# A long convolution with a spectral mix on one core: another layout for the last sequence's u, an earlier identity load and fewer zero columns

## The chip, the cores and the metric

The kernel runs on one core of one Trainium2 chip. The metric is the device time of one execution in microseconds (us), and a time shown alone is the median of its runs. The engines are called as in the profile: PE (TensorE, matrix multiplication), PEld (its weight loads), DVE (VectorE), ACT (ScalarE), POOL (GpSimd) and SP (SyncE, which here issues DMA transfers only). PSUM is the memory that TensorE writes to; an "evacuation" is the copy by VectorE or ScalarE of a result from PSUM to SBUF.

## The reference

Inputs are x (8, 5696, 128), h (5696, 128), two sets of 64 complex mixing matrices (w_r and w_i, each 64, 128, 128) and w_ch (128, 128), all float32. Two functions follow each other:

```python
def _attn_ref(x, h):                       # causal long convolution
    B, S, D = x.shape
    L = 2 * S
    Xf = np.fft.rfft(x, n=L, axis=1)
    Hf = np.fft.rfft(h, n=L, axis=0)
    Yf = Xf * Hf[None, :, :]
    y = np.fft.irfft(Yf, n=L, axis=1)[:, :S, :]
    return y.astype(np.float32)

def _moe_ref(x, w_r, w_i, w_ch):           # x is the y from above
    B, S, D = x.shape
    n_modes = w_r.shape[0]                 # 64
    X = np.fft.rfft(x, axis=1)
    Y = np.zeros_like(X)
    Xr, Xi = (np.real(X[:, :n_modes]), np.imag(X[:, :n_modes]))
    Yr = np.einsum('bmd,mde->bme', Xr, w_r) - np.einsum('bmd,mde->bme', Xi, w_i)
    Yi = np.einsum('bmd,mde->bme', Xr, w_i) + np.einsum('bmd,mde->bme', Xi, w_r)
    Y[:, :n_modes] = Yr + 1j * Yi
    y = np.fft.irfft(Y, n=S, axis=1)
    u = x + y
    return (u + np.maximum(u @ w_ch, 0.0)).astype(np.float32)
```

## The kernel before, in words

**Order and semaphores.** The kernel is a list of operations for each engine, written out by hand. A recorder (`Recorder`, L21 to L121) keeps them in the order of the program text, and works out semaphores from tokens: an operation names the tokens that it reads and writes, and with `after=` those whose earlier readers and writers must be done. There is no scheduler, so an engine runs its operations strictly in the order in which the text adds them. Helpers record nearly everything: `evac` (L304, with the ScalarE copies at L311 and L313 and the VectorE ones at L315 and L317), `dma` (L319, issue at L320) and `mm` (L322, matmul at L323). Transfers issued by SP or by POOL go out in the order of that engine.

**Sizes.** A sequence has S = 5696 = 64 x 89 positions. A position is written J·q + p with J = 64, NQ = 89 values of q and p from 0 to 63. There are NK = 90 frequency groups k, 0 to 89. The eight sequences are worked in NP = 4 pairs. The frequencies go in NT = 23 ticks (steps) of KT = 4 k each.

**First stage.** The first transform is along q. `F1` (L142) holds its 90 cosines and 90 sines as 2·NK = 180 columns, of which the imaginary ones of k = 0 and k = 89 are zero. The filter h is transformed first, in 16 tiles (`Ah`). Then `a_tile` (L461) does the same for a pair: four matmuls F, Xin of 180 columns into two PSUM banks, and one evacuation with a scale of 1/64 into `As` (128 partitions x 720 elements). A pair has 32 such tiles, and where nothing else is said VectorE and ScalarE take them by turns.

**Ticks.** `tick` (L650) does, for four k: `second` (L606), matmuls As, M of 128 columns that finish the transform; `products` (L617), the product with the transformed filter `Hs` on VectorE, into `U`; two steps later the first half of the inverse transform, U times Wc, evacuated by ScalarE into a buffer `Zs` or `Zt` and stored to DRAM (`zscr`) by a transfer on SP; and one step after that the matmuls G, Zs, which gather the 64 lowest modes of y in one PSUM bank, MB. The function `zroom` (L645) says which buffer a step uses; in the last pair, step 21 uses the buffer of step 13, so ScalarE's cast of step 21 waits until step 13's store has landed.

**Between the pairs.** While the last ticks of a pair run, tiles 0 to 5 of the next pair's first stage are put among them (`border`, L556). Tiles 6 to 31 follow between the pairs (L741): odd ones are evacuated by VectorE, even ones by ScalarE, and the last one is split between both. After them the next pair's `second` begins.

**The last pair's extra work.** Among its ticks the transfers for the output stage are issued by the dictionary `early` (L557): for example, at tick 14 `load_id` and `clear_zt(1)`, at tick 15 `load_zt(1, "gpsimd")` (1 MB, `ZT1a`), at tick 16 and 18 the tables `S4a` and `IBs`. All of these are POOL's, but for the identity matrix `Id`, which `load_id` (L568) puts on SP, with a wait (`after=ZY`) for the stores of steps 8 and 9, whose buffers lie in the same memory.

**Mix and output stage.** `mix` (L806) multiplies the modes by the weights `W`, and eight transposes with `Id` (L824) bring the result to `C`. Then `u_tile` (L787) makes u: for each sequence four chunks of 16 values of p, each chunk in two halves; a half is two PSUM banks, each with eight matmuls S4, ZT of 89 columns (the inverse transform of the convolution, read back from `zscr`) and one IBs, C of 356 columns (the mix). It is evacuated to `UT`, one 5696-column row for each of the 128 channels, with the positions in their natural order. `o_tile` (L841) makes a piece of the result: four matmuls UT, WI of 256 columns, with 128 columns of `UT` as weights each time and WI = [w_ch, identity] as the moving side, so that PSUM holds u @ w_ch beside u with positions on the partitions; ScalarE takes the maximum with 0 (L871) into `R`, VectorE adds u (L872) into `O`, and SP sends it out (L883). A sequence has eleven tiles of four groups of 128 columns, in pairs of 4 KB a row (1024 float32), and 64 positions that are left go as a short tile for two sequences together. A list `todo` (L885) deals output tiles out between the u tiles of the following pair. In the last pair all of sequence 6 comes before sequence 7, and with its last u tile twelve whole output tiles and a short one are still to be done, since every output tile of the old layout takes its columns from all four chunks:

```python
lh = bass.AP(u_sb[ub], 4 * r4 + j, [[S, P], [NW, P]])      # column 44*i + 4*r4 + j, i = 0..127
```

Of the kernel before, what the change touches and what calls it, by code (L numbers as in the profile page):

```python
# [4 lines left out]
P = 128  # L5
# [118 lines left out]
def bass_long_conv_fft__then__afno_spectral_mix_kernel(nc, x, h, moe_w_r, moe_w_i, moe_w_ch, out):  # L124
# [3 lines left out]
    J = 64  # L128
# [13 lines left out]
    f1 = np.zeros((P, 2 * NK))  # L142
    f1[0:NQ] = np.stack([fwd.real, fwd.imag], axis=2).reshape(NQ, 2 * NK)
# [105 lines left out]
    f1_sb = at("F1", 2 * NK, F16, take(2 * NK * 2))  # L249
# [13 lines left out]
    assert 2 * S + 8 * ZP <= AW * 2  # L263
# [19 lines left out]
    id_sb = at("Id", P, F16, r_off[1])  # L283
# [63 lines left out]
    R.add("scalar", lambda e: e.copy(zf, ap(f1_sb, 2 * NK, J, P - J, 1, [[0, XW // 2]])), [("f1",)], [("xz",)])  # L347
# [69 lines left out]
    dma("sync", wc_sb[:, :], bass.AP(c_w, 0, [[3 * P, P], [1, 2 * P]]), "c", (), [("wc",)])  # L417

# [13 lines left out]
    for i in range(WARM):  # L432
        mm(pv(6 + i % 2, 0, [[1, 2 * NK]]), f1_sb[:, 0:P], f1_sb[:, :], True, True, [("f1",)], [bank(6 + i % 2)])
# [6 lines left out]
    for j in range(16):  # L440
        t = turns("h", [0, 2, 4])
        for i in range(4):
            d = 4 * j + i
            mm(pv(t + i // 2, (i % 2) * 2 * NK, [[1, 2 * NK]]),
               ap(hp_sb, 2 * J * HS, 0, P, d, [[HS, 2 * J]]), f1_sb[:, :], True, True,
               [("hz",), ("hp", d // DC), ("f1",)], [bank(t + i // 2)])
        for i in range(4 if j < 15 else 26):
            mm(pv(6 + i % 2, 0, [[1, 2 * NK]]), f1_sb[:, 0:P], f1_sb[:, :], True, True, [("f1",)], [bank(6 + i % 2)])
        evac(bass.AP(ah_sb, 4 * j, [[HW, P], [DH, 2 * NK], [2, 2], [1, 2]]),
             pv(t, 0, [[1, 2 * NK], [512, 2], [2 * NK, 2]]),  # L450
             [bank(t), bank(t + 1)], [("ah", j)], 1.0 / 64,
             eng="vector" if j in (3, 7) else "scalar")
# [8 lines left out]
    def a_tile(j, slots, eng=None):  # L461
        t = turns("s", slots) if len(slots) > 1 else slots[0]
        for i in range(4):
            d = 4 * j + i
            mm(pv(t + i // 2, (i % 2) * 2 * NK, [[1, 2 * NK]]),
               ap(x_sb, XW, 0, P, d, [[XS, 2 * J]]), f1_sb[:, :], True, True,
               XIN + XZ + [("f1",)], [bank(t + i // 2)])
        if eng == "both":
            for i, e in enumerate(("vector", "scalar")):
                evac(bass.AP(a_sb, 4 * j + 2 * i, [[AW, P], [D, 2 * NK], [1, 2]]), pv(t + i, 0, [[1, 2 * NK], [2 * NK, 2]]),  # L470
                     [bank(t + i)], [("as", j + i)], 1.0 / 64, eng=e, after=once(("hp", j), HP))
            return
        evac(bass.AP(a_sb, 4 * j, [[AW, P], [D, 2 * NK], [2, 2], [1, 2]]),
             pv(t, 0, [[1, 2 * NK], [512, 2], [2 * NK, 2]]),
             [bank(t), bank(t + 1)], [("as", j)], 1.0 / 64, eng=eng, after=once(("hp", j), HP))


# [8 lines left out]
    def filter_tick(t, banks):  # L486
        n = len(ticks[t])
        hb = banks
        for i, k in enumerate(ticks[t]):
            for r in range(2):  # L490
                for dh in range(2):
                    mm(pv(hb[dh], i * DH, [[1, DH]]),
                       ap(m_sb, MW, J * dh, J, k * 3 * J + (J if r == 0 else 0) + dh * J, [[1, P]]),
                       ap(ah_sb, HW, J * dh, J, (2 * k + r) * DH, [[1, DH]]), r == 0, r == 1,
                       AHT + mtok(k) + [("ag", k)], [bank(hb[dh])])
# [54 lines left out]
    def load_s4(part):  # L550
# [9 lines left out]
             14: lambda: (load_id(), clear_zt(1)),  # L560
# [14 lines left out]
    def keep(n, b0):  # L575
        for i in range(n):
            mm(pv(b0 + i % 2, 0, [[1, 2 * NK]]), f1_sb[:, 0:P], f1_sb[:, :], True, True, [("f1",)], [bank(b0 + i % 2)])
# [28 lines left out]
    def second(g_, t):  # L606
        sl = slot_of(g_, t)
        for i, k in enumerate(ticks[t]):
            for r in range(2):
                for b in range(2):  # L610
                    col = k * 3 * J + (J if r == 0 else 0) + b * J
                    mm(pv(sl + b, i * D, [[1, D]]),
                       ap(m_sb, MW, J * b, J, col, [[1, P]]),
                       ap(a_sb, AW, J * b, J, (2 * k + r) * D, [[1, D]]), r == 0, r == 1,
                       AST + mtok(k), [bank(sl + b)])
# [139 lines left out]
    LSLOT = [0, 2, 4, 6]  # L755
    NCH = J // ZB
# [30 lines left out]
    def u_tile(i, b, half):  # L787
# [4 lines left out]
        else:  # L792
            for hb in range(2):
# [6 lines left out]
        evac(bass.AP(u_sb[ub], c_ * ZB + half * 8, [[S, P], [J, NQ], [4, 2], [1, 4]]),  # L800
             src, [bank(t), bank(t + 1)], [("u_", ub, 2 * c_ + half)], eng=e, after=once(("u", ub), old))
# [39 lines left out]
    def o_tile(g_, b, r4):  # L841
# [19 lines left out]
        n, rows = (4, P) if full else (2, TAIL)  # L861
        rd = [("u_", v_, c_) for v_ in ubs for c_ in range(2 * NCH)] + [("wch",), ("i16",)]
# [8 lines left out]
        R.add("scalar", lambda e: e.activation(rv, src_r, RELU), bk, [("r", i % NR)], after=once(("r", i % NR), G_ALL + XTT + [("y", 0), ("y", 1), ("id",)]))  # L871
# [5 lines left out]
        if full:  # L877
            dst = bass.AP(out.tensor, out.offset + bb * S * D + (4 * r4 - 4 * h_) * D, [[NW * D, P], [1, w_]])
            src = ob[:, 0:w_]
        else:  # L880
            dst = bass.AP(out.tensor, out.offset + bb * S * D + NW * P * D, [[D, TAIL], [S * D, 2], [1, D]])
            src = bass.AP(ob, 0, [[OW, TAIL], [D, 2], [1, D]])
# [56 lines left out]
```

## Time and profile before

| | |
|---|---|
| median of 3 runs | 385.36 us (384.66 to 386.22) |
| the profiled execution | 387.21 us |
| span of that execution in the trace | 385.1 us |
| mean granted TensorE clock | 0.98 |
| busy, share of the span | PE 94%, PEld 73%, DVE 77%, ACT 82%, POOL 22% |
| moved by DMA | 103.94 MB, mean 270 GB/s |
| output of u and results (290 to 372 us) | PE busy 81.93 of 82.00 us |

The profile is of one execution, somewhat slower than the median of the timed runs. The span runs from the first instruction to the last event; the 2.1 us between it and the execution's own time lie around it. Times in rows of the trace are counted from the start of the span. A row of a group gives the line, the engine, the operation with output and inputs and their shapes, the number of instructions, and in brackets the idle time of the engine just before them with what ended it. "SPq" and "POOLq" are the queues in which these engines issue transfers. The clock column is the TensorE clock that was granted, as a share of full speed.

### The profile page before, as it was taken

How to read it: one execution, taken by the hardware profiler on the slowest of the kernel's cores; microseconds unless marked ns; L12 is line 12 of the kernel's file. 1: busy time of each engine (PE TensorE's matmuls, PEld its weight loads, DVE VectorE, ACT ScalarE, POOL GpSimd, SP SyncE). 2: the span in 40 equal slices, each digit the busy share in tenths (PEclk: the TensorE clock that was granted, in tenths of full speed). 3: DMA queues.
4: the chain of work that ended last, by engine and by line, in shares of the span. 5: the costliest groups of instructions: out<-in, count | busy, mean ns of one | idle time of the engine just before them, and what ended most of it. 6: DMA issues, size and time to landing. Idle time of an engine off the chain costs nothing.

```text
span 385.1 us, 12438 instructions
## 1 busy us (share of the span) xinstructions
PE 362.4 (94%) x5346; PEld 280.7 (73%) x5346; DVE 296.6 (77%) x336; ACT 314.3 (82%) x491; POOL 85.2 (22%) x134
## 2 busy tenths in 40 slices
PE   7989899999989999999999899978999999999994
PEld 7878766667856667756667666648789989888873
DVE  3649899988988998989999988761537767766665
ACT  8469699898989997899998899965447777688884
POOL 8812012100733311823203213307200000000000
PEclk9999999999999999999999999995799999999999
DMA  7999969977999995999995799999999999999877
GB/s 148 206 298 354 243 139 249 250 220 222 97 126 215 249 268 151 132 134 232 243 274 114 95 325 357 327 367 292 392 391 362 367 416 403 419 405 383 325 293 316
DMA packets 87137, 103.94 MB, mean 270 GB/s; under 512 B 22819, under 2 KB 72611, under 8 KB 83527
## 3 DMA queue, kind: packets, MB, share of 16 engines
q1 hardware_dynamic: 62603, 67.76, 50.7%
q0 software_dynamic: 24480, 35.40, 44.2%
q8 instruction: 42, 0.69, 0.7%
q14 instruction: 12, 0.10, 0.1%
HBM read 70.61 MB, written 51.12 MB: 316 GB/s over the span
## 4 chain that ended last, share of the span: by engine, by line
PE 76%; DMA 8%; DVE 6%; ACT 4%; POOL 3%; issue 2%; DVEq 0%; ACTq 0%; POOLq 0%
PE ps L323 76%; DMA Xr<-in_x_dram 4%; DMA zscr<-Zs 3%; DVE As L317 2%; DVE U L630 2%; POOL Xr L320 2%; ACT As L313 2%; ACT R L871 1%; POOL Hin L320 1%; DVE Xin L365 1%; DVE Hs L315 1%; ACT Zt L311 1%; ACT Zs L311 0%; DMA Hs<-Hs 0%; ACT Xs L311 0%
## 5 line engine op out<-in xcount | busy, mean ns | idle before, releaser
L323 PE MATMUL ps<-U,Wc 128*128 128x512 f16 (+1 forms) x368 | 94.4, 377 | 4.2 <-ACT Zs L311 3.7
L638 DVE TENSOR_TENSOR U<-Xs,Hs 128x2048 f16<-128x2048 f16 (+1 forms) x73 | 86.9, 1192 | 13.8 <-ACT Xs L311 13.1
L311 ACT CAST Xs<-ps 128x1024 f16<-128x1024 f32 (+1 forms) x77 | 75.1, 979 | 12.6 <-PE ps L323 7.6
L311 ACT CAST Zs<-ps 128x512 f16<-128x512 f32 (+1 forms) x132 | 69.3, 592 | 5.5 <-DMA zscr<-Zs 3.8
L872 DVE TENSOR_TENSOR O<-ps,R 128x512 f32<-128x512 f32 x81 | 52.3, 685 | 20.1 <-ACT R L871 11.2
L317 DVE TENSOR_SCALAR As<-ps 128x720 f16<-128x720 f32 x70 | 57.7, 886 | 5.2 <-PE ps L323 4.6
L871 ACT ACTIVATE R<-ps 128x512 f32<-128x512 f32 (+1 forms) x92 | 50.5, 591 | 8.5 <-PE ps L323 8.4
L323 PE MATMUL ps<-F,Xin 128*128 128x180 f16 x512 | 53.7, 249 | 3.9 <-DVE Xin L365 2.6
L323 PE MATMUL ps<-As,M 64*128 64x128 f16 x1440 | 50.3, 217 | 3.5 <-DVE U L630 2.9
L323 PEld LDWEIGHTS ps<-F,Xin 128*128 128x128 f16 x512 | 44.4, 155 | 12.6 <-DVE As L317 2.8
L323 PEld LDWEIGHTS ps<-U,Wc 128*128 128x128 f16 x368 | 28.6, 97 | 33.3 <-ACT Zs L311 7.6
L313 ACT ACTIVATE As<-ps 128x720 f16<-128x720 f32 (+1 forms) x61 | 45.7, 769 | 7.9 <-PE ps L323 6.5
L323 PE MATMUL ps<-WI,UT 128*128 128x256 f16 x360 | 51.1, 278 | 0.5 <-ACT UT L311 0.4
L311 ACT CAST UT<-ps 128x712 f16<-128x712 f32 x46 | 34.5, 752 | 19.2 <-PE ps L323 18.0
L323 PEld LDWEIGHTS ps<-As,M 64*128 64x128 f16 x1440 | 40.6, 94 | 9.7 <-DVE U L630 3.6
L323 PEld LDWEIGHTS ps<-WI,UT 128*128 128x128 f16 x360 | 39.1, 152 | 3.4 <-issue 1.8
L323 PE MATMUL ps<-IBs,C 128*128 128x356 f16 x128 | 40.3, 324 | 0.1
L320 POOL DMA_DIRECT2D Xt<-in_x_dram x40 | 21.1, 533 | 80.8 <-PE ps L323 80.3
L323 PEld LDWEIGHTS ps<-G,Zs 128*128 128x128 f16 x512 | 26.3, 97 | 14.3 <-ACT Zs L311 1.6
L638 DVE TENSOR_TENSOR U<-ps,Hs 128x2048 f16<-128x2048 f32 x15 | 34.3, 2284 | 0.0
L323 PE MATMUL ps<-G,Zs 128*128 128x128 f16 (+2 forms) x512 | 32.4, 193 | 0.0
L311 ACT CAST Zt<-ps 128x512 f16<-128x512 f32 x52 | 28.5, 624 | 0.3 <-PE ps L323 0.3
(88 smaller groups left out, 504.7 us busy)
## 6 DMA issues: line engine op xcount, KB each, us to landing
out_dram<-O SPq DMA_DIRECT2D x39, 512.0 KB, 7.6
zscr<-Zs SPq DMA_DIRECT2D x62, 256.0 KB, 7.0
zscr<-Zt SPq DMA_DIRECT2D x26, 256.0 KB, 6.8
Xt<-in_x_dram POOLq DMA_DIRECT2D x20, 320.0 KB, 7.1
W<-wscr POOLq DMA_DIRECT2D x4, 1024.0 KB, 8.2
M<-cM POOLq DMA_DIRECT2D x5, 720.0 KB, 16.9
ZT0a<-zscr SPq DMA_DIRECT2D x3, 1024.0 KB, 8.8
Hs<-Hs SPq DMA_DIRECT2D x44, 64.0 KB, 6.3
```

What stands on the lines that cost most here:

```text
L311: R.add(e, lambda h_: h_.copy(dst, src), reads, writes, after=after)
L313: R.add(e, lambda h_: h_.activation(dst, src, COPY, scale=scale), reads, writes, after=after)
L315: R.add(e, lambda h_: h_.tensor_copy(dst, src), reads, writes, after=after)
L317: R.add(e, lambda h_: h_.tensor_scalar_mul(dst, src, scale), reads, writes, after=after)
L320: R.add(eng, lambda h_: h_.dma_start(dst, src), reads, writes, ring=ring, after=after)
L323: R.add("tensor", lambda h_: h_.matmul(o, l, r, start=st, stop=sp), reads, writes)
L365: R.add("vector", lambda e: e.tensor_copy(bass.AP(x_sb, i * XN * XS, [[XW, NQ], [XS, XN], [1, D]]), src), list(toks) + XZ, [("xin", i)])
L630: R.add("vector", lambda e, b=b, s_=s_: e.tensor_tensor(bass.AP(u_s[i], b * 512, [[2048, P], [1024, 2], [1, n * D]]), s_, hv, MULT), [tok, ...
L638: R.add("vector", lambda e: e.tensor_tensor(uv, src, hv, MULT), bk + [("h", t, 0), ("h", t, 1, 0), ("h", t, 1, J)], [("u", i)])
L871: R.add("scalar", lambda e: e.activation(rv, src_r, RELU), bk, [("r", i % NR)], after=once(("r", i % NR), G_ALL + XTT + [("y", 0), ("y", 1 ...
L872: R.add("vector", lambda e: e.tensor_tensor(ov, src_u, rv, ADD), bk + [("r", i % NR)], [key + (h_,)], after=once(key, old))
```

## The change

Four things are changed, and all of them keep what is computed.

1. **Zero columns.** The two zero columns of F1 are left out (NF = 178 for 180). The evacuations write from the second group of `Ah` and `As` on, and the matmuls of `second` and of the filter that multiplied by the two zero groups (k = 0 and k = 89, imaginary) are not issued.
2. **Identity.** `Id` lies in the free end of the `As` region, and is loaded by SP right behind Wc at the start, without a wait; it is no longer among the early actions at tick 14.
3. **Shares of the first stage.** Between the pairs the 25 whole tiles 6 to 30 go by a pattern of nine, five to ScalarE and four to VectorE: 14 and 11, where it was 13 and 12. The first pair's 31 whole tiles go by a string, 16 to ScalarE and 15 to VectorE, and tile 31 is split between both.
4. **The last sequence.** For sequence 7 the columns of `UT` are in another order: first by halves of p (0 to 31, 32 to 63), then by bit jh of p, then q, then four runs of four positions. One half needs chunks 0 and 1 alone, the other 2 and 3. Each half gives six output tiles, of 32, 32 and 25 values of q with two tiles each; a tile's rows are (q, run), 128, 128 or 100 of them. The first ten tiles go out in pairs with 4 KB a row, the last two singly with 2 KB a row. The 64 positions left of sequence 6 are a short tile of its own. Output tiles are dealt out two after the first and three after the second half of each u chunk of the last pair, and the first six tiles of sequence 7 are put on the list two chunks before the end.

In the order of the instructions, TensorE's UT, WI matmuls are 363 after and 360 before; 40 of them stand behind the last matmul of u, where 50 stood.

The core of the diff:

```diff
-    f1 = np.zeros((P, 2 * NK))
-    f1[0:NQ] = np.stack([fwd.real, fwd.imag], axis=2).reshape(NQ, 2 * NK)
+    NF = 2 * NK - 2
+    f1 = np.zeros((P, NF))
+    f1[0:NQ] = np.delete(np.stack([fwd.real, fwd.imag], axis=2).reshape(NQ, 2 * NK), [1, 2 * NK - 1], axis=1)
...
-    id_sb = at("Id", P, F16, r_off[1])
+    id_sb = at("Id", P, F16, a_as + (2 * NK - 1) * D * 2)
...
     dma("sync", wc_sb[:, :], bass.AP(c_w, 0, [[3 * P, P], [1, 2 * P]]), "c", (), [("wc",)])
+    dma("sync", id_sb[:, :], bass.AP(c_w, 2 * P, [[3 * P, P], [1, P]]), "c", (), [("id",)])
...
-        evac(bass.AP(a_sb, 4 * j, [[AW, P], [D, 2 * NK], [2, 2], [1, 2]]),
-             pv(t, 0, [[1, 2 * NK], [512, 2], [2 * NK, 2]]),
+        evac(bass.AP(a_sb, D + 4 * j, [[AW, P], [D, NF], [2, 2], [1, 2]]),
+             pv(t, 0, [[1, NF], [512, 2], [NF, 2]]),
...
+    def group(k, r):
+        return 2 * k + r if k else 1
+
+    def parts_of(k):
+        return (0,) if k in (0, NK - 1) else (0, 1)
...
         for i, k in enumerate(ticks[t]):
-            for r in range(2):
+            for r in parts_of(k):
...
-             14: lambda: (load_id(), clear_zt(1)),
+             14: lambda: clear_zt(1),
...
-    def load_id():
-        dma("sync", id_sb[:, :], bass.AP(c_w, 2 * P, [[3 * P, P], [1, P]]), "c", (), [("id",)], after=ZY)
...
+    SHARE = [V if c_ == "V" else A for c_ in "VAVAAVAVAVAVAVAVAVAAVVAVAVAVAVA"]
     for j in range(32):
-        a_tile(j, FOUR)
+        a_tile(j, FOUR, "both" if j == 31 else SHARE[j])
...
-                a_tile(j, [(4, 6, 0, 2)[(j - 7) % 4] if j > 6 else 0], "both" if j == 31 else V if j % 2 else A)
+                a_tile(j, [(4, 6, 0, 2)[(j - 7) % 4] if j > 6 else 0], "both" if j == 31 else (A, V)[(j - 6) % 9 % 2])
...
+    QG, QA8 = P // 4, J // 16
...
+        if (g_, b) == (NP - 1, 1):
+            dst = bass.AP(u_sb[ub], c_ // 2 * NQ * (J // 2) + (c_ % 2 * 2 + half) * 4, [[S, P], [4 * QA8, NQ], [4 * QA8 * NQ, 2], [1, 4]])
...
-        full = r4 < NW // 4
-        ubs = [ub] if full else [ub, ub + 1]
         last_ = (g_, b) == (NP - 1, 1)
-        wide = r4 < (8 if last_ else NW // 4 // 2 * 2)
-        big = wide or (last_ and full)
+        full = last_ or r4 < NW // 4
+        ubs = [ub] if full or g_ + 1 == NP else [ub, ub + 1]
+        if last_:
+            hf, qg, jh = r4 // 6, r4 % 6 // 2, r4 % 2
+            nq = min(QG, NQ - QG * qg)
+            p_at = J * QG * qg + J // 2 * hf + 4 * jh
+        wide = r4 < (10 if last_ else NW // 4 // 2 * 2)
+        big = wide or last_
...
+        n, rows = (4, nq * QA8 if last_ else P) if full else (len(ubs), TAIL)
+        rd = [("u_", v_, c_) for v_ in ubs for c_ in (range(NCH * hf, NCH * hf + NCH) if last_ else range(2 * NCH))] + \
+             [("wch",), ("i16",)]
         for j in range(n):
-            lh = bass.AP(u_sb[ub], 4 * r4 + j, [[S, P], [NW, P]]) if full else u_sb[ubs[j]][:, NW * P:S]
+            if last_:
+                lh = bass.AP(u_sb[ub], ((2 * hf + jh) * NQ + QG * qg) * QA8 * 4 + j, [[S, P], [4, rows]])
...
+        if last_:
+            dst = bass.AP(out.tensor, out.offset + (bb * S + p_at - 4 * h_) * D, [[J * D, nq], [8 * D, QA8], [1, w_]])
+            src = ob[0:rows, 0:w_]
...
-                for _ in range((2, 2 + half)[n >= NCH] if last else 1 + half):
+                for _ in range(2 + half if last else 1 + half):
...
             if last and n == NCH - 1:
-                todo += [(g_, 0, r4) for r4 in range(NW4)]
-        todo += [(g_, 0, NW4)] * last
-        todo += [(g_, b, r4) for b in range(1 if last else 0, 2) for r4 in range(NW4)]
-        todo += [(g_, 0, NW4)] * (not last)
+                todo += [(g_, 0, r4) for r4 in range(NW4 + 1)]
+            if last and n in (NCH + 1, 2 * NCH - 1):
+                todo += [(g_, 1, r4) for r4 in range(6 * (n > NCH + 1), 6 + 6 * (n > NCH + 1))]
+        if not last:
+            todo += [(g_, b, r4) for b in range(2) for r4 in range(NW4)] + [(g_, 0, NW4)]
```

More of the change, by code (lines that the diff above doesn't have):

```diff
@@ L248, in bass_long_conv_fft__then__afno_spectral_mix_kernel @@
           [at(f"Zt{i}", 1024, F16, a_g + GW * 2 + i * 2048) for i in range(NZX - NZ)]
-    f1_sb = at("F1", 2 * NK, F16, take(2 * NK * 2))
+    f1_sb = at("F1", NF, F16, take(NF * 2))
     wc_sb = at("Wc", 2 * P, F16, take(2 * P * 2))
@@ L262, in bass_long_conv_fft__then__afno_spectral_mix_kernel @@
               (a_m2, a_g)]
-    assert 2 * S + 8 * ZP <= AW * 2
+    assert 2 * S + 8 * ZP <= (2 * NK - 1) * D * 2 and 2 * XC * XB * 2 <= (2 * NK - 1) * D * 2
     zt = [[at(f"ZT{i}{'ab'[p_]}", ZP, F16, zt_off[i][p_]) for p_ in range(2)] for i in range(NC)]
@@ L608, in second @@
         for i, k in enumerate(ticks[t]):
-            for r in range(2):
+            for r in parts_of(k):
                 for b in range(2):
@@ L799, in u_tile @@
         src = pv(t, 0, [[1, NQ], [512, 2], [NQ, 4]])
-        evac(bass.AP(u_sb[ub], c_ * ZB + half * 8, [[S, P], [J, NQ], [4, 2], [1, 4]]),
-             src, [bank(t), bank(t + 1)], [("u_", ub, 2 * c_ + half)], eng=e, after=once(("u", ub), old))
+        dst = bass.AP(u_sb[ub], c_ * ZB + half * 8, [[S, P], [J, NQ], [4, 2], [1, 4]])
+        if (g_, b) == (NP - 1, 1):
+            dst = bass.AP(u_sb[ub], c_ // 2 * NQ * (J // 2) + (c_ % 2 * 2 + half) * 4, [[S, P], [4 * QA8, NQ], [4 * QA8 * NQ, 2], [1, 4]])
+        evac(dst, src, [bank(t), bank(t + 1)], [("u_", ub, 2 * c_ + half)], eng=e, after=once(("u", ub), old))
     XTT = [(n, g_) for g_ in range(NP) for n in ("xt", "xtn")]
@@ L860, in o_tile @@
         OW = 1024 if big else 512
-        n, rows = (4, P) if full else (2, TAIL)
-        rd = [("u_", v_, c_) for v_ in ubs for c_ in range(2 * NCH)] + [("wch",), ("i16",)]
+        n, rows = (4, nq * QA8 if last_ else P) if full else (len(ubs), TAIL)
+        rd = [("u_", v_, c_) for v_ in ubs for c_ in (range(NCH * hf, NCH * hf + NCH) if last_ else range(2 * NCH))] + \
+             [("wch",), ("i16",)]
         for j in range(n):
-            lh = bass.AP(u_sb[ub], 4 * r4 + j, [[S, P], [NW, P]]) if full else u_sb[ubs[j]][:, NW * P:S]
+            if last_:
+                lh = bass.AP(u_sb[ub], ((2 * hf + jh) * NQ + QG * qg) * QA8 * 4 + j, [[S, P], [4, rows]])
+            else:
+                lh = bass.AP(u_sb[ub], 4 * r4 + j, [[S, P], [NW, P]]) if full else u_sb[ubs[j]][:, NW * P:S]
             mm(pv(t + j // 2, (j % 2) * 256, [[1, 256]], 0, rows), lh, WI, True, True, rd, [bank(t + j // 2)])
@@ L880, in o_tile @@
         else:
[L881 to L882 removed]
+            dst = bass.AP(out.tensor, out.offset + bb * S * D + NW * P * D, [[D, TAIL], [S * D, n], [1, D]])
+            src = bass.AP(ob, 0, [[OW, TAIL], [D, n], [1, D]])
         dma("sync", dst, src, "o", [key + (v_,) for v_ in range(h_ + 1)])
```

26 lines of the change are left out of this document (13 added, 13 removed).

## The prediction

> **What bounds the kernel now.** I read the slices of the page first, then the busy time by stage, the chain of waits, and the timeline where the chain leaves TensorE. The stages, from the windows (us, PE, PEld, DVE, ACT, POOL busy, clock, DMA share, GB/s):
>
> ```profile
> 92.00:109.00 17.00, 15.51 (x196) 13.19 (x198) 15.16 (x19) 14.40 (x23) 9.63 (x13) 1.00 1.02 125
> ...
> 248.00:261.00 13.00, 9.92 (x139) 5.99 (x136) 7.49 (x6) 9.07 (x17) 0.80 (x2) 0.98 1.03 355
> 261.00:272.00 11.00, 10.17 (x200) 9.53 (x201) 2.70 (x5) 5.78 (x8) 9.76 (x11) 0.50 0.98 324
> ...
> 290.00:372.00 82.00, 81.93 (x1128) 72.71 (x1126) 57.64 (x89) 64.41 (x112) 0.00 (x0) 1.00 0.95 377
> 372.00:385.00 13.00, 7.13 (x50) 5.18 (x48) 8.08 (x14) 7.91 (x14) 0.00 (x0) 0.93 0.80 316
> ```
>
> TensorE fills the output stage (81.93 of 82.00), so every matmul added there is paid. Two places are not TensorE's: the middle, 248 to 272, with an idle stretch and then half the clock, and the last 13 us. The chain passes through one store in the middle, and the timeline says what held it:
>
> ```profile
> 247.65 0.20 ACT Zs L311
> 247.86 13.02 DMA zscr<-Zs
> 260.88 0.02 issue
> ```
>
> ```profile
> 247.48 0.33 SPq L320 DMA_DIRECT2D Id<-cW  x1
> ...
> 247.86 3.37 SPq L320 DMA_DIRECT2D zscr<-Zs  x3
> ...
> 251.27 7.15 SPq L320 DMA_DIRECT2D zscr<-Zt  x2
> ...
> 260.96 1.66 ACT L311 CAST Zs<-ps 128x512 f16<-128x512 f32 x4 [3.78 <-DMA zscr<-Zs]
> 261.60 0.61 PE L323 MATMUL ps<-U,Wc 128*128 128x256 f16 x2 [3.68 <-ACT Zs L311]
> ```
>
> The Id load waits on SP for the stores of steps 8 and 9 to land (the second at 247.465). Step 13's data was cast by 245.55, but its store stands behind Id and went out at 247.86, as POOL's 1 MB and 0.7 MB loads (ZT1, S4a, IBs) filled the engines. Step 21 reuses that buffer, so ACT stood 3.78 us and TensorE 3.68 us, and the clock was 0.50 from 260.40 to 274.05.
>
> **The middle: Id leaves SP's queue at step 14.** The store can go out at about 245.6 to 247.1 in place of 247.86, and ACT needs it landed at 257.2. Its sixteen landings came from 255.08 to 260.88, nine by 256.75. In the packets, an engine serves the two queues by turns: an 8 KB packet of POOL's (0.305 us), then one of SP's (512 B, 0.023). On a typical engine five or six of the 8 KB packets ran alone before Id's eight packets came, so the store moves up by about 13 of its 32 packets: on those engines it ends before IBs begins. On the slowest, POOL's 28 packets follow each other until 260.2, and 32 turns need nearly all of that. Bounds: 0 (the slowest engine decides as before) and -6.2. The second is the whole gap, 3.7, and the clock, about 2.5: seven 356-column matmuls at 0.295 in place of 0.15 (1.0), five blocks of eight 89-column ones at 0.07 in place of 0.0425 (1.1), 128 small ones at 0.030 in place of some 0.027 (0.4). I take landing near 259, about the middle: the gap falls to some 2 us (-1.5), and since the clock fell 2.48 us after the last matmul's end (257.92), it stays up (-2.5): **-4.0**. What is late next is S4a (landed 258.6), in time for that. [...]
>
> **The border between pairs: 13 and 12 whole tiles become 14 and 11.** Before, by engine:
>
> ```profile
> 97.41 9.28 ACT L313 ACTIVATE As<-ps 128x720 f16<-128x720 f32 x12 [0.27 <-PE ps L323]
> ```
>
> ```profile
> 97.10 9.52 DVE L317 TENSOR_SCALAR As<-ps 128x720 f16<-128x720 f32 x12 [0.19 <-PE ps L323]
> ```
>
> VectorE is the bound: it starts a whole tile every 0.815 us without a gap, eleven from 97.10 to 106.07 (8.97). ScalarE can start one every 0.674 (95.69 to 96.37). After, of the same stretch VectorE has ten and ScalarE twelve, each 1% shorter (712 columns for 720): 10 x 0.806 = 8.06 and 12 x 0.667 = 8.0. At best -0.9; two ScalarE tiles in a row with four PSUM slots in fixed order can take it all back, so 0 to -0.9, and I take the middle: 3 x -0.45 = **-1.35**. The first pair's tiles (27 to 43.5) get the same kind of share, 15 and 16 with the last split; VectorE ends at 43.39 and the 16 filler matmuls at 43.6, which follow the last tile by 1.35 us whatever happens. 0 to -0.8, taken -0.35.
>
> **Dropped columns.** Four matmuls fewer in each pair and four in the filter, 20 at 0.028 to 0.034: 0 to -0.6, taken -0.3. The F matmuls lose two of 180 columns (0.0773 us apart): under 1 ns each, behind the evacuation. **Id at the start** puts eight 256 B packets on each engine while the chain runs through Xr's landing (to 26.24): at most 8 x 0.027, +0.1.
>
> **The last pair.** Before, after the last matmul of u (371.82) twelve whole tiles and one short one are left; VectorE takes one every 0.6 us and ends at 381.22:
>
> ```profile
> 374.55 6.67 DVE L872 TENSOR_TENSOR O<-ps,R 128x512 f32<-128x512 f32 x11 [0.18 <-issue]
> ```
>
> ```profile
> 365.56 7.20 SPq L320 DMA_DIRECT2D out_dram<-O  x5
> 374.08 0.98 SPq L320 DMA_DIRECT2D out_dram<-Os  x2
> 375.87 5.89 SPq L320 DMA_DIRECT2D out_dram<-O  x7
> ```
>
> After, ten are left (four of the first half, six of the second), and the first four need not wait for the last cast: about 1.45 + 10 x 0.6 = 7.5 us for 9.4, so -1.9. But 13 more output matmuls lie before that point (three more in all, ten moved), in a stage that TensorE fills: 13 x 0.13 (eight took 1.06 to 1.14) = +1.7. Together **-0.2**, bounds -0.8 (weights read at 8 bytes' stride load faster than at 88: 0.152 against 0.097 for contiguous rows) and +0.4.
>
> **The last transfers.** Rows are now (q, four runs); a third of each half's rows is 25 x 4 = 100. The DMA issues before:
>
> ```profile
> ZT0b<-zscr SPq DMA_DIRECT2D x3, 416.0 KB
> ```
>
> ```profile
> out_dram<-O SPq DMA_DIRECT2D x11, 512.0 KB, 3.3
> out_dram<-O SPq DMA_DIRECT2D x3, 256.0 KB, 3.4
> ```
>
> Every SP transfer of 128 or 64 rows signalled 16 landings. ZT0b, of 52 rows, has no landing time because it signalled one event 0.57 us after its issue and then 13: it ran on 13 engines, which divides 52. Of 100 rows against 25 on the other side, 5 is the share that divides both; 10 divides only one. A 4 KB packet takes 0.155 us and a 2 KB one 0.080. On five engines: tiles 4 and 5 take 20 x 0.155 = 3.1 (for 1.24), tiles 10 and 11 each 20 x 0.08 = 1.6 (for 0.64). Measured from VectorE's end T, with 0.85 us from issue to first packet: tiles 4 and 5 run from T-2.6 to T+0.5, the two pairs after them to T+3.0, the last two to T+6.2, landed T+6.5. Before it was 384.66 - 381.22 = 3.44. **+3.05** on five engines; on ten, the same working gives T+3.4, so 0. I take five. [...]
>
> **Sum.** -4.0 - 1.35 - 0.35 - 0.3 + 0.1 - 0.2 + 3.05 = -3.05. The profiled execution took 387.21 (span 385.1, 2.1 around it); the median shown is 385.36. So 384.2 for an execution like the profiled one, and **382.3** for the median. A measurement of this kernel can tell about 0.5%, 1.9 us, from no change.
>
> **Rivals.** *The store lands as late as before.* For: SP's issue of the fifth store in flight took 6 us (the 251.27 line), so step 13's, fifth behind steps 9 to 12, may be held till about 247.1 anyway; the slowest engine was late through an instruction fetch of 0.88 us at 250.38, which no part of the change removes. Against: the eight Id packets and the idle turns are gone. Middle -0.5 in place of -4.0: +0.45, 385.8.
>
> *The last transfers use ten engines or more.* For: 100 rows on the SBUF side divide by ten, and no row shows unequal sides. Against: 25. Without the 3.05: -6.1, 379.3.
>
> *Slower: the five engines decide.* Place: the last 8 us, where three transfers of the five-engine kind queue with two of the others. Price 3.05, and 3.75 if the engine that lagged 0.68 us at the end (384.66 against 383.98) is one of the five. It decides from the point where all that comes before gives less than that. With the middle at 0 and the border half as good it is +3.75 - 0.7 - 0.3 - 0.2 + 0.1 = +2.65, 388.0. For: both larger gains hang on waits that I could not bound away from zero. Against: VectorE's share at the border is plain.
>
> **Chances.** Forecast 0.36, store late 0.27, ten engines 0.19, slower 0.18. Faster by over 0.5%: forecast (382.3 lies below 383.4) and ten engines, less a little for a weaker border: 0.52. Within: the late store and that rest, 0.31. Slower: 0.17. The range leaves out a tenth at each end: 378.6, somewhat under the ten engines, to 387.6, just under the slower rival.
>
> **What would show it.** Right: the Id row beside Wc at the start; no wait of ACT on the zscr store above 2 us near 257, and the clock at 1.00 through the middle; border evacuation ending some 0.45 us sooner after its first tile; ten output tiles after the last u; five landings and one early event for the 100-row transfers, and over 6 us from VectorE's last tile to the end of the span. Wrong: a clock of 0.50 after the middle's gap, sixteen or ten landings for 100 rows, or ScalarE late at the border's end.

## The result

The changed kernel is slower: 393.35 us in the median of 6 runs (391.95 to 396.21) against 383.99 of 6 runs of the kernel before (381.70 to 386.22), a ratio of 1.025 with a 95% interval of 1.021 to 1.029. Its profiled execution took 393.65 us with a span of 391.4; that of before 387.21 with 385.1. The stages of the changed kernel, from its windows (us, PE, PEld, DVE, ACT, POOL busy, clock, DMA share, GB/s):

```profile
92.00:109.00 17.00, 15.43 (x198) 13.18 (x198) 14.83 (x19) 14.63 (x24) 9.56 (x13) 1.00 1.02 132
248.00:261.00 13.00, 12.66 (x193) 8.34 (x192) 8.82 (x8) 12.43 (x22) 5.20 (x9) 1.00 1.08 373
261.00:272.00 11.00, 8.29 (x158) 7.01 (x155) 5.05 (x5) 3.31 (x5) 5.78 (x6) 0.70 1.01 383
290.00:372.00 82.00, 81.91 (x1110) 72.39 (x1108) 58.16 (x90) 64.60 (x113) 0.00 (x0) 1.00 0.96 378
372.00:392.00 20.00, 5.63 (x46) 4.18 (x42) 6.78 (x12) 6.33 (x11) 0.00 (x0) 0.73 0.46 162
```

The idle stretch of 248 to 261 is gone (12.66 busy of 13 for 9.92), but in the next row TensorE is busy 8.29 of 11, for 10.17 before. The last row has become 7 us longer, at a DMA share of 0.46 for 0.80.

Put side by side event by event, the two profiled executions differ like this (a minus is earlier after the change):

| up to | difference, us | of this stage |
|---|---|---|
| VectorE's first product U | -0.21 | -0.21 |
| the 21st product of pair 0 | +0.38 | +0.59 |
| the first product of pair 3 | +0.28 | -0.10 |
| XT of the last pair | -3.74 | -4.02 |
| the first half of Y | -4.08 | -0.34 |
| the second half of Y | -1.65 | +2.43 |
| the ninth evacuation of u | -1.77 | -0.12 |
| VectorE's last result tile | -1.54 | +0.23 |
| the end of the span | +6.34 | +7.88 |

The -0.10 between pair 0 and pair 3 is three borders (-0.43, -0.44 and -0.40) against a longer wait for a transfer of x at 200.4 (1.6 us of TensorE's time; at most 1.3 in the other profiles). The border's evacuations, from ScalarE's and VectorE's timelines, now end at 106.71 and 106.51:

```profile
97.74 8.97 ACT L314 ACTIVATE As<-ps 128x712 f16<-128x712 f32 x13 [0.28 <-PE ps L324]
...
97.43 9.08 DVE L318 TENSOR_SCALAR As<-ps 128x712 f16<-128x712 f32 x11 [0.19 <-PE ps L324]
```

Before, VectorE took twelve in that row and ended at 106.62, though it had begun 0.33 sooner. In the middle, SP issued the store of step 13 at 245.86 (247.86 before; it is the second of the four in SP's row), its last landing came at 250.65 (260.88 before), and ScalarE's timeline shows no wait on it:

```profile
243.89 5.50 SPq L321 DMA_DIRECT2D zscr<-Zs  x4
...
256.34 2.65 ACT L312 CAST Zs<-ps 128x512 f16<-128x512 f32 x6
259.39 0.38 ACT L314 ACTIVATE XT<-ps 128x256 f16<-128x256 f32 x1 [0.40 <-PE ps L324]
```

Two rows of the table decide: +7.88 behind VectorE's last tile, and +2.43 inside the mix. For the first, the timeline, SP's waits, and the transfers from 372 to 392 in 40 slices of 0.5 us:

```profile
373.61 6.07 DVE L889 TENSOR_TENSOR O<-ps,R 128x512 f32<-128x512 f32 x10 [0.91 <-PE ps L324]
```

```profile
SPq L928 <- DMA out_dram<-O: 5.9, 1, 5.9
```

```profile
GB/s 373 242 0 33 418 426 172 0 319 434 295 123 57 90 213 197 328 344 401 418 369 148 131 98 41 82 119 70 94 98 111 86 41 29 25 25 25 8 0 0
...
out_dram<-O SPq DMA_DIRECT2D x4, 512.0 KB, 4.7
out_dram<-O SPq DMA_DIRECT2D x1, 400.0 KB
out_dram<-O SPq DMA_DIRECT2D x2, 200.0 KB
```

VectorE is done at 379.68, 1.5 us sooner than before, and the span ends 11.73 us later, where it was 3.85. The three transfers of 100 rows (400 and 200 KB) have no landing time, as they signalled one early event and five more each. With five engines at work the rate falls to about 100 GB/s, and the last 2.5 us run at 25 GB/s: one engine alone, at 2 KB in 0.084 us.

For the second, the timeline of TensorE (in brackets: idle before the instruction, and what ended it):

```profile
266.30 1.26 PE L324 MATMUL ps<-XT,W 128*128 128x16 f16 x37 [2.48 <-issue]
```

It stands in the middle of the mix, between two matmuls with the same inputs, and no semaphore ended it. The trace has a queue called "instruction" with 42 packets of 16,384 bytes, and 10,770 records of TensorE, some 256 for each packet. Counted over TensorE's records, the first matmul after the gap is number 7617, which is 193 modulo 256; a packet for it began at 263.99 and took 0.94, and TensorE went on 1.37 us after its end. A smaller gap of 1.08 us in pair 0, at 68.59, stands at number 1985, also 193 modulo 256. When the packets of all 17 profiles are matched in order with the borders at 193 modulo 256, no block's first instruction ran sooner than 2.19 us after its packet had started (697 borders), and at this gap it was 2.31. TensorE waited for its own instructions.

### The profile page after: what moved, and what is told of

It reads as the page before. It is cut to its first block, busy times and chain, and to the rows that moved or that the text cites. A ratio compares the mean times of both kernels' runs of the same rounds, so it can differ in the third digit from the quotient of the medians.

```text
span 391.4 us, 12411 instructions
## 1 busy us (share of the span) xinstructions
PE 358.3 (92%) x5329; PEld 277.8 (71%) x5329; DVE 296.6 (76%) x334; ACT 314.1 (80%) x496; POOL 84.1 (21%) x134
## 4 chain that ended last, share of the span: by engine, by line
PE 71%; ACT 8%; DMA 6%; DVE 6%; issue 3%; POOL 3%; DVEq 0%; POOLq 0%
PE ps L324 71%; ACT As L314 6%; DMA Xr<-in_x_dram 4%; DMA Xt<-in_x_dram 2%; DVE As L318 2%; DVE U L635 2%; POOL Xr L321 2%; ACT Zs L312 1%; POOL Hin L321 1%; DVE Xin L366 1%; DVE Hs L316 1%; DMA Hs<-Hs 0%; ACT R L888 0%; ACT Xs L312 0%; PE ps L833 0%
## 5 line engine op out<-in xcount | busy, mean ns | idle before, releaser
L889 DVE TENSOR_TENSOR O<-ps,R 128x512 f32<-128x512 f32 (+1 forms) x82 | 53.1, 685 | 20.8 <-ACT R L888 11.2
L318 DVE TENSOR_SCALAR As<-ps 128x712 f16<-128x712 f32 (+1 forms) x67 | 55.1, 873 | 5.7 <-PE ps L324 4.0
L888 ACT ACTIVATE R<-ps 128x512 f32<-128x512 f32 (+3 forms) x93 | 50.7, 590 | 8.6 <-PE ps L324 8.4
L324 PE MATMUL ps<-F,Xin 128*128 128x178 f16 x512 | 51.9, 248 | 5.1 <-DVE Xin L366 3.7
L324 PE MATMUL ps<-WI,UT 128*128 128x256 f16 (+1 forms) x363 | 51.3, 277 | 0.6 <-DVE O L889 0.5
L314 ACT ACTIVATE As<-ps 128x712 f16<-128x712 f32 (+1 forms) x65 | 45.5, 762 | 7.2 <-PE ps L324 6.6
L324 PEld LDWEIGHTS ps<-WI,UT 128*128 128x128 f16 (+1 forms) x363 | 39.0, 149 | 3.9 <-issue 1.6
```

The costliest lines, as they stand in the source:

```text
L314: R.add(e, lambda h_: h_.activation(dst, src, COPY, scale=scale), reads, writes, after=after)
L318: R.add(e, lambda h_: h_.tensor_scalar_mul(dst, src, scale), reads, writes, after=after)
L324: R.add("tensor", lambda h_: h_.matmul(o, l, r, start=st, stop=sp), reads, writes)
L889: R.add("vector", lambda e: e.tensor_tensor(ov, src_u, rv, ADD), bk + [("r", i % NR)], [key + (h_,)], after=once(key, old))
```

## The experiments

All ratios are against runs of the kernel before in the same series. Those runs lie between 381.3 and 387.3 us. Theory A: the last transfers run on few engines, a number that divides the rows of both sides as the 13 of ZT0b's landings divides its 52 rows, and the end waits for them. Rival B: the new rows' addresses, 32 KB apart, are slow whatever carries them. Theory D, after the first series: dropping columns moves the borders of TensorE's instruction blocks to a place where the fetch comes late.

**1. The 100-row transfers in two** (e1_split): 64 rows, which 16 divides, and 36, which nine divides on both sides.

```diff
-            dst = bass.AP(out.tensor, out.offset + (bb * S + p_at - 4 * h_) * D, [[J * D, nq], [8 * D, QA8], [1, w_]])
-            src = ob[0:rows, 0:w_]
+            for q0, q1 in ([(0, nq)] if nq == QG else [(0, 16), (16, nq)]):
+                dma("sync", bass.AP(out.tensor, ... + J * q0) * D, [[J * D, q1 - q0], [8 * D, QA8], [1, w_]]), ob[q0 * QA8:q1 * QA8, 0:w_], ...)
+            return
```

> The changed kernel, but each transfer of 100 rows is issued as two, of 16 and 9 values of q (64 and 36 rows). Theory A (few engines: the 100-row transfers run on five of the sixteen engines, and the end waits for these): 16 and 9 landings, and from VectorE's last result tile to the end of the span about 4.5 us in place of 11.7, so some 7 us less than the changed kernel, near 386 us or 1.005 of the kernel before. Rival B (addresses: rows 32 KB apart make the writes slow, whatever engines carry them): packets of 4 KB above 0.25 us stay as frequent at the end, and the end stays above 8 us, so about 391 us.

Measured: 385.49 us, 1.008 (1.003 to 1.012). 16 landings and nine; from VectorE's last tile to the end 5.13 us for 11.73. Theory A holds for the larger part of the loss. With nine engines at work some packets are slow too: 44 of the 490 packets of 4 KB from 4 us before VectorE's end on took over 0.2 us, where 0.159 is usual. The gap in the mix is there again (2.22 us, at 7617).

**2. The 25-q tiles first in each half** (e4_25_first): `hf, qg, jh = r4 // 6, (r4 % 6 // 2 + 2) % 3, r4 % 2`.

> The changed kernel with the tiles of 25 values of q first in each half, so that the last transfers have 128 rows; the transfers of 100 rows stay whole. Theory A (five engines hurt where nothing hides them): still five landings for 100 rows, but from VectorE's last tile to the end about 5 us (their packets are done about 3.2 us after it), so 6 us less than the changed kernel, near 387 us. Rival B (addresses): the end stays above 8 us.

Measured: 390.97 us, 1.016 (1.010 to 1.023); the end takes 9.18 us, nearer to B's figure than to A's 5. The transfers of 100 rows still had five landings. They hurt although they are no longer last, and 80 of 554 packets of 4 KB in the end took over 0.2 us, the longest 0.879, where 0.159 is usual. So the count alone does not explain it, and B was not out yet.

**3. The kernel before's own rows on five engines** (g3_before_125): layout and addresses untouched, three transfers issued as 125 and 3 rows.

```diff
+            if last_ and r4 in (7, 9, 10):
+                for p0, p1 in ((0, 125), (125, P)):
+                    dma("sync", bass.AP(out.tensor, ..., [[NW * D, p1 - p0], [1, w_]]), ob[p0:p1, 0:w_], ...)
+                return
```

> The kernel before with three of its last five whole transfers (the fourth pair of 4 KB rows and the last two of 2 KB rows) issued as 125 rows and 3 rows; layout and addresses stay. 125 is divided by no number from 6 to 16, so by the rule of theory A the large part runs on five engines. Theory A: one early event and five landings for each, and from VectorE's last tile to the end about 8.6 us in place of 3.4 to 3.9 (25 packets of 0.159, then 16 of 0.084 shared and twice 25 of 0.084, on the same five engines), so the kernel is 4 to 5 us slower, 1.011 to 1.013. If their packets also take 1.3 to 2 times as long, as in the changed kernel, the slowness belongs to few engines and the end is above 10 us. Rival B (addresses 32 KB apart): packets stay at 0.159 and 0.084, and only the count costs.

Measured: 392.55 us, 1.023 (1.018 to 1.029). Each 125-row transfer had one early event and five landings. The transfers from 372 to 392:

```profile
GB/s 410 180 62 260 416 442 418 418 402 418 410 107 94 127 115 180 184 168 102 86 82 94 61 94 86 123 111 82 115 107 131 127 102 57 29 25 25 0 0 0
...
out_dram<-O SPq DMA_DIRECT2D x1, 500.0 KB
out_dram<-O SPq DMA_DIRECT2D x2, 250.0 KB
```

The same picture: some 100 GB/s, then 25. The end takes 13.1 us where the count alone gives 8.6. While five engines carry the large parts, 38 packets of 4 KB and 94 of 2 KB took over 1.25 times the usual; in the 4 us after VectorE's last tile it was on average 1.5 times for 4 KB and 2.3 times for 2 KB. In the two profiles of the kernel before, with these transfers on 16 engines, none took above 0.2 us in the last 4 us of VectorE's work and after it. So B falls as the cause: the slower packets come with few engines at the old addresses too. Whether the new addresses add to it is not shown, since no run has them with 16 engines alone, and why the packets get slower is open.

**4. The front alone** (e2_old_tail): the changed kernel with the last pair of before.

> The changed kernel with the last pair's layout, dealing and transfers of the kernel before; zero columns, the early Id and the shares of the first stage stay. Theory A: all of the loss is in the left-out part, so this is faster than the kernel before: about -1.3 (three borders at 0.43), -0.2 (first stage), -1.9 to -4 (middle), together 0.989 to 0.993 of it. Rival: the dropped columns or shares cost elsewhere (pair 0 and pair 2 of the changed kernel's trace lost 0.6 and 1.1 us against before), and the ratio is 0.997 or above.

Measured: 388.68 us, 1.012 (1.006 to 1.018). This was the surprise: the three edits meant for the front lose together. The profiled execution has a gap of 2.82 us in the mix, again at 7617.

**5. Id back at tick 14** (e3_old_tail_id14).

```diff
+             14: lambda: (load_id(), clear_zt(1)),
```

> As e2_old_tail, but Id is loaded at tick 14 behind the stores of steps 8 and 9, as before. Theory (Id alone held up step 13's store): TensorE's gap of some 3.7 us before step 21's products with Wc and the half clock after it come back, and the time is 2 to 4 us above e2_old_tail, near 0.996 of the kernel before. Rival (the transfers of POOL decide, or instruction blocks give it back): no difference above 1 us.

Measured: 387.70 us, 1.008 (1.004 to 1.013): not slower than 4. Its profile has a gap of 2.30 us for step 13's store, and that of 4, with Id early, one of 2.15. So the theory that Id alone held up the store gets no support.

**6. The kernel before, once more** (b1_before_again).

> The kernel before, unchanged, for a second profile: the profiled execution of 387.21 us lies above all but few of the timed ones (381.5 to 386.2). Theory C (the stall on step 13's store belongs to slow executions of the kernel before): at about 383 us the gap before step 21's products is under 2.5 us and the clock after it stays at 1.00, so the middle takes some 4 us less than in the first profile. Rival: the gap of 3.7 us is there again, and the difference lies elsewhere.

Measured: 387.32 us, with the gap (2.69 us) again, so this run told nothing of theory C by itself. The answer came from runs 3, 7 and 9, which have the code of before up to there, or nearly: in their profiles TensorE has no gap there (none above 0.15 us).

**7. The shares alone** (x1_shares_only).

```diff
-        a_tile(j, FOUR)
+        a_tile(j, FOUR, "both" if j == 31 else SHARE[j])
...
-   ... "both" if j == 31 else V if j % 2 else A)
+   ... "both" if j == 31 else (A, V)[(j - 6) % 9 % 2])
```

> The kernel before with the shares of the first stage alone (nine by nine, five to ScalarE, between the pairs; the string in the first pair). Theory: each border ends 0.43 us sooner, the first stage 0.2, nothing else moves: -1.5 us, 0.996 of the kernel before. Rival D (work that comes earlier meets transfers and instruction blocks that do not): 1.000 or above.

Measured: 381.79 us, 0.995 (0.990 to 1.000). The first two borders gain 0.26 each (0.44 with the shorter tiles of the full change). Its profiled execution, 380.73 us, has neither gap, and the middle of it shows what an execution without them looks like. The clock falls to 0.50 even here, from 263.76 to 267.18:

```profile
248.00:261.00 13.00, 12.66 (x228) 8.99 (x225) 9.25 (x8) 12.31 (x20) 6.18 (x8) 1.00 1.05 376
261.00:272.00 11.00, 10.51 (x193) 9.04 (x190) 5.34 (x7) 3.88 (x6) 4.26 (x6) 0.84 1.01 388
```

**8. The zero columns alone** (x2_columns_only): 20 matmuls fewer, evacuations 1% shorter, nothing else.

> The kernel before with the two zero columns of F1 left out and nothing else: 20 matmuls fewer, each evacuation of a first-stage tile 1% shorter; Id is loaded at tick 14 into its old place. Theory D (20 matmuls fewer move the borders of the blocks of 256 TensorE instructions, so that one falls where its fetch comes late): slower than the kernel before by 1 to 4 us, with a gap of 2 us or more in the mix at an instruction whose number is 193 modulo 256. Rival: -0.3 us, no such gap that the kernel before does not have.

Measured: 388.11 us, 1.010 (1.006 to 1.014). Less work makes the kernel slower. TensorE's timeline:

```profile
268.54 1.23 PE L324 MATMUL ps<-XT,W 128*128 128x16 f16 x37 [3.31 <-issue]
```

**9. The columns, with 20 warming matmuls more** (f2_columns_warm112): `WARM = 112` for 92, done while TensorE waits at the start, so that later instructions have their old numbers.

> x2_columns_only with 20 more warming matmuls (112), which puts the blocks back where they were by the middle. Theory D: the gap in the mix is gone and the time is that of the kernel before or up to 1 us less (0.997 to 1.000). Rival: still 1.010.

Measured: 383.90 us, 1.000 (0.996 to 1.003). The gap in the mix is gone, and so is that for the store in this profile. The clock fell all the same, to 0.50 from 264.28 to 271.10:

```profile
260.00:265.00 5.00, 4.80 (x150) 4.81 (x150) 3.30 (x3) 2.93 (x2) 5.00 (x7) 0.93 1.06 410
265.00:270.00 5.00, 4.77 (x39) 3.54 (x37) 2.69 (x4) 2.00 (x3) 1.72 (x1) 0.50 1.03 377
```

**10. The kernel before, with 20 warming matmuls fewer** (f1_before_warm72): `WARM = 72`, nothing else.

> The kernel before with 20 warming matmuls fewer at the start (72 for 92) and nothing else: every later TensorE instruction moves 40 places forward against the blocks of 256, as the dropped columns move it by the middle. Theory D: a gap of 2 us or more opens in the mix at an instruction that is 193 modulo 256, as in x2_columns_only, and the kernel gets slower by 2 to 4 us (1.006 to 1.010). Rival: the columns themselves cost, the place of the blocks does not: within 1 us of the kernel before.

Measured: 388.30 us, 1.012 (1.008 to 1.017). Its timeline has both gaps, the store's and that of the mix, at number 7617:

```profile
261.02 0.39 PE L323 MATMUL ps<-U,Wc 128*128 128x256 f16 x2 [3.01 <-ACT Zs L311]
...
270.50 1.19 PE L323 MATMUL ps<-XT,W 128*128 128x16 f16 x34 [3.00 <-issue]
```

Runs 9 and 10 settle theory D: no column is touched in 10, and only the place of the blocks differs. The shorter warming itself cost nothing: VectorE's first product U came at 43.92 us, against 44.18 and 43.87 in the two profiles of before. What the traces show around the border, for some of the runs (time of TensorE's instruction 7361, where the block before begins; how much later the 16 KB packet started; TensorE's wait at 7617):

| kernel | 7361 at | packet | wait |
|---|---|---|---|
| kernel before | 257.24 | +2.24 | none |
| x1_shares_only | 256.00 | +2.43 | none |
| f2_columns_warm112 | 257.47 | +2.45 | none |
| changed kernel | 259.04 | +4.95 | 2.48 |
| e1_split | 257.41 | +4.61 | 2.22 |
| x2_columns_only | 259.75 | +6.55 | 3.31 |
| f1_before_warm72 | 262.06 | +6.16 | 3.00 |

The other ten profiles: e2_old_tail, e4_25_first and g1_zt3_late, with the blocks of the changed kernel, have +5.66, +4.81 and +4.87 and waits of 2.82, 2.23 and 2.01; in b1, e7, f3, f4, g2 and g3, with the blocks of before, the packet came at +2.2 to +2.6, and there is no wait. e3_old_tail_id14 has the blocks of the changed kernel, but its packet came at +2.93, just in time; its profile lost 1.1 us at number 8897 in the output stage instead, which is 193 modulo 256 too.

**11. The whole front and the split, with the blocks put back** (e7_split_warm112: e1_split with `WARM = 112`).

> e1_split with 20 more warming matmuls at the start, where TensorE waits 1.8 us for the filter's load: every later TensorE instruction has the number (of 64 bytes in blocks of 256) that it had before the zero columns were dropped. Theory D: the 2.2 us gap in the mix gets smaller or goes and its half clock with it, 2 to 4 us less than e1_split. Rival: the gap stays, since the mix (128 matmuls within 4 us) reads blocks faster than they arrive wherever the border lies; no difference above 1 us.

Measured: 384.15 us, 1.000 (0.996 to 1.004), no gap at 7617. Theory D again; with the blocks mended and 16 and nine engines, the change is worth nothing.

**12. The front with the blocks put back, Id early or at tick 14** (f3_old_tail_warm112, f4_old_tail_id14_warm112).

> e2_old_tail with 112 warming matmuls: shares, dropped columns and the early Id, with the old last pair. Theory D: the mix's gap of 2.8 us goes, 1.0118 becomes 0.990 to 0.995 (the shares' -1.5 us, and -1 to -2 more if Id's place keeps the store of step 13 from coming late in some executions). Rival: above 1.000.

> As f3_old_tail_warm112 with Id loaded at tick 14 behind the stores of steps 8 and 9. If Id's place matters, this is 1 to 3 us above f3_old_tail_warm112 and shows more executions of the longer kind; if the transfers of POOL alone decide when step 13's store lands, the two agree within 0.5 us.

Measured: 383.77 us, 1.000 (0.997 to 1.004), and 384.43 us, 1.001 (0.997 to 1.005). The gap in the mix is gone in both, but 1.000 is more than the 0.990 to 0.995 expected. The place of Id makes 0.7 us at most, within the noise. In the profiles the store's gap is 1.90 with Id early and 2.26 with Id late.

**13. A lighter load at the fetch** (g1_zt3_late, g2_shares_zt3_late): ZT3 loaded after the ticks, in 4 and in 7.

> e2_old_tail with POOL's two loads of ZT3 (1.4 MB) issued after the ticks, behind those of WI, in place of right behind ZT2's. Theory E (the fetch of the block that begins at TensorE's instruction 7617 is late because it is asked for as POOL's 2.8 MB of ZT2 and ZT3 go out): its packet starts under 4 us after instruction 7361 in place of 5.7, the gap in the mix shrinks from 2.8 to under 1, and the kernel gains 1 to 3 us on e2_old_tail (1.003 to 1.009). Rival (a fetch comes late under any load): gap of 2 us or more as before.

> x1_shares_only with the same later loads of ZT3. Theory E: x1_shares_only has no gap in the mix, so nothing is gained there: 0.995, and 0.992 if the second, longer kind of execution gets rarer. Rival (ZT3 is then late for u's fourth chunk): TensorE waits near the thirteenth evacuation of u, slower than x1_shares_only by over 1 us.

Measured: 386.52 us, 1.006 (1.003 to 1.010), and 381.92 us, 0.998 (0.995 to 1.000). In the first the time lies in the range that theory E gave, but what it gave for the fetch did not come: the packet started 4.87 us after 7361 (forecast: under 4) and the wait was 2.01 (forecast: under 1). Theory E is not borne out, and what delays the fetch stays open. In the second, u lost nothing by the later load, and nothing was gained that is clear of the noise.

The fastest kernel seen is x1_shares_only, the share of tiles alone; its interval just touches 1.

## Why the prediction was wrong, step by step

Between the two profiled executions the forecast was -3.05 and the outcome +6.34. Of the 9.39 us between them, 4.83 are the last transfers (+7.88 for +3.05), 2.1 the mix (+2.43 and -0.34, where nothing was forecast), 1.25 the stretch with the three borders (-0.10 for -1.35) and 0.6 pair 0 (+0.59, where nothing was forecast). The medians lie 3 us further apart, because the profiled execution of before took 3.2 us more than the median of its six runs (see the middle).

**"Dropped columns ... taken -0.3"** is the step whose sign was wrong. It measured +1.0% (run 8), some 3.8 us. I priced the instructions that go, and not that all others move against the blocks of 256. The 16 KB packets were in the trace, and the rival about the late store names one; I saw them only as a load on a DMA engine. The price that the traces show is the wait (2.0 to 3.3 us). The clock was at 0.50 from 265.32 to 272.15 in the changed kernel, but for as long, 6.83 us, in f2 and g3, which have no gap; so the half clock is not shown to be a part of the price.

**"The last transfers ... +3.05"** had the right mechanism and the right number of engines, five; the size was wrong: +7.88. The number was an estimate from ZT0b's 13 landings for 52 rows, with no transfer of unequal sides to go by; the three transfers of 100 rows had five landings each behind the early event. The prediction put the last landing at T+6.5, and the end came at T+11.73. Three things are missing in it: the first packets of tiles 4 and 5 started 0.5 us later (377.6); packets got slower while few engines worked (63 of the 484 packets of 4 KB from 4 us before T on took over 0.2 us, the longest 0.848; from T-2 to T+2 they took 1.3 times the usual on average); and one of the five ended its packets at 390.68, 2.3 to 3 us after the other four (an instruction packet of 0.95 us went through at 377.74; the trace does not say on which engine). The usual packets take 0.159 and 0.084 us in the trace, where the sum has 0.155 and 0.080; that is 0.3 us of it. The rival "slower: the five engines decide" had this place, with a price of 3.75 at most.

**"The middle ... -4.0"** has its number met by the two profiled executions up to XT (-4.02), but by luck: the parts are others. Forecast were a store that lands near 259, a gap that shrinks by 1.5, and 2.5 for a clock that stays up. The store landed at 250.65, the whole gap of 3.68 went, and the clock did not stay up. It fell to 0.50 near this place in all 17 profiles: for 13.65 us in both of before, f1, e2 and x2, 10.24 in e3, f3, f4, g1 and g2, 6.83 in the changed kernel, e1, e4, e7, f2 and g3, and 3.41 in x1; f2, g3 and x1 have neither gap. So the prediction's reading, that the clock fell because of the gap, is not borne out; it was only longer at 0.50, for 10.24 us or more, in the ten profiles with a gap of over 1 us for the store. Nor did the clock carry that price: from XT to the ninth evacuation of u it took 16.60 us before, 16.68 in f2, 16.64 in g3 and 15.56 in x1.

Id's place was not shown to be the cause of the gap either. With Id at tick 14, TensorE's gap for step 13's store was 3.68, 2.69, 3.01, 2.30, 2.26, 1.36 and 1.22 in seven profiles (the kernel before twice, f1, e3, f4, x2 and g2) and absent in three (x1, f2, g3); with Id early it was 2.15, 1.90, 1.16 and 0.88 in four (e2, f3, g1, e7) and absent in three (changed, e1, e4). A small part for Id is not excluded by these counts. The gap comes and goes: g3 has the code of before up to there and no gap, and the spread of the times of before (381.3 to 387.3) fits that. I took a wait in one execution for a property of the kernel, and forecast a gain on the median from it. As the profiled execution lay 1.9 us above the shown median, the profile was a slower one; I noted that and drew nothing from it.

**"The border ... 3 x -0.45"** held: from VectorE's 21st product to the 25th it took 22.29 us before and 21.86 after, -0.43, and -0.44 at the second border; the shares alone gave -0.26 (run 7), the shorter tiles alone -0.20 (run 9). **The first stage** gave -0.21 for -0.35.

**"The last pair ... -0.2"** came to +0.23. The last matmul of u moved from 371.82 to 372.07, while the stage had begun 1.77 earlier: +2.0 for the added output matmuls, for 1.7. The way from there to VectorE's end got 1.8 shorter, for 1.9. Weights of `UT` at 8 bytes' stride loaded in 0.113 us for 128 columns, against 0.149 at 88 bytes' in the kernel before, but those of 100 columns in 0.168.

Added up, the separately measured parts are +3.8 (columns), -1.9 (shares), about 0 (Id) and +5.1 (last pair and its transfers, from 1.012 to 1.025): +7.0 of the 9.4 measured. The rest lies within their intervals, each about 0.5% to each side, and is not explained further.

## What to carry to other kernels

Transfers of 100 rows against 25 x 4 ran on five engines here, and their cost at the end of the kernel was more than packets times their usual time (+7.88 us, forecast +3.05): choose row groups by what divides both sides, or split them (64 and 36 rows: 5.13 us to the end for 11.73). When an edit adds or drops instructions on an engine that lives from a dense stream, look at where the blocks of 256 fall; a changed number of warming matmuls tells in one run whether a loss comes from there (1.010 went back to 1.000 in run 9). And a gap in one profiled execution, above all one slower than the median, needs a second profile before anything is forecast from it.

## What the runs showed of the hardware

- TensorE's instructions came in 42 packets of 16,384 bytes, one for 256 of its records. At the border in the mix a packet started 2.2 to 6.6 us after the first instruction of the block before was executed; over all borders of the 17 profiles it was from 1.2 us before it to 7.5 us after it. In the mix, where TensorE had to wait, it went on 1.3 to 1.5 us after the packet's end. Shifting the stream by 40 instructions cost 1.2% (f1).
- With transfers on five engines, packets of 4 KB took on average 1.3 times their usual 0.159 us in the changed kernel, over a stretch of 4 us; in g3, with the old addresses, those of 4 KB took 1.5 times, and those of 2 KB 2.3 times their usual 0.084 us. In the changed kernel the five finished up to 3 us apart.
- The granted clock fell to 0.50 around the end of the last pair's ticks (at 259.2 to 265.3 us) in every profile, for 3.41 to 13.65 us, with and without a gap on TensorE, and was then at 1.00 for 109.23 us in each of the 17.
- The 100-row transfers with sides of 100 and 25 x 4 used five engines by their landings, 36 rows of 9 x 4 nine (e1), 125 rows five (g3), and ZT0b's 52 rows 13 (the kernel before). Each of these numbers divides the rows of both sides.
